# A linear-attention and Fourier-mixing kernel on one core: tiles loaded as 96 and 16 rows, a second copy of half the values, the token fold on VectorE, and a new order of steps

## The chip, the core and the metric

The kernel runs on one core of one Trainium2 chip. Five engines work side by side, each through its own queue in order: TensorE (PE; its weight loads are shown as PEld), VectorE (DVE), ScalarE (ACT), GpSimd (POOL) and SyncE (SP), which here only issues DMAs. They wait for one another by semaphores. The metric is the device time of one execution in microseconds; less is better. Before the change it was 549.24 us, the median of three runs (547.84 to 549.38).

## What is computed

Attention with a decaying state, for 4 batches of 8 heads, 768 tokens and 48 channels:

```python
f = 1.0 / (1.0 + np.exp(-f_logit))
state = np.zeros((B, H, D, D), dtype=np.float32)
for t in range(S):
    state = f[:, :, t, :, None] * state + np.einsum('bhd,bhe->bhde', k[:, :, t], v[:, :, t])
    y[:, :, t] = np.einsum('bhd,bhde->bhe', q[:, :, t], state)
```

The heads' outputs stand beside one another as x (4 x 768 x 384), and the second part is

```python
X = np.fft.fft(np.fft.fft(x, axis=1), axis=2)
u = x + np.real(X)
un = (u - mean(u)) / np.sqrt(var(u) + 1e-06)
return u + np.maximum(un @ w_ch1, 0.0) @ w_ch2
```

with w_ch1 of 384 x 1536 and w_ch2 of 1536 x 384, given as 64-bit floats.

## The kernel before

**Units.** The attention goes by 16 units, each a pair of heads of one batch (unit u is batch u // 4, pair u % 4). A tile of queries, keys or factors has the channels on the partitions and the 768 tokens along the row: one head on rows 0 to 47, the other on rows 64 to 111[...]. Rows 48 to 63 belong to no head; they are filled once (`gap`, L130, and the fills in `start`, L137) so that instructions over all 112 rows read something harmless. The DRAM array holds, for each unit, the two heads' channels one after the other. `load` (L162) brings each tile in as two DMAs of 48 rows. There are four tiles of factors (`g_t`), four of queries (`q_t`) and three of keys (`k_t`), used in turn.

**Steps of a unit** (`attention`, L332, then `outputs`, L511, and `fold`, L613), each ended by a `yield`: (1) exponential and logarithm of the factor on ScalarE; (2) on VectorE a scan over the tokens in six chunks of 128 (L347) and the chunk ends `deep` (L348), of which the sixth column is a copy on GpSimd (L349); (3) three exponentials; (4) queries and keys times decay on VectorE (L359, L361, L362); (5) scores of each chunk's two halves of 64 against themselves, on TensorE (L370); (6) a masked copy (L374); (7) values times these weights, and the far scores, second half of a chunk against the first (L545); (8) the remaining values (L528) and products of keys with values (L565) from keys turned by the word `K` (L507); (9) the scan over chunk states (L573); (10) states into outputs (L582) and five copies; (11) turning back into tokens by channels (L602); (12) and (13) the token fold: sums and differences of token rows that the Fourier part needs.

The far scores of chunks 0 to 2 come out on partitions 0 to 63, those of chunks 3 to 5 on 64 to 127. [...] Before, the halves of chunks 3 to 5 are exchanged for this: in the values by their loads (L169, L171), in the keys by a second multiply that writes in exchanged order (L362).

In `fold` the name `other` (L628) is GpSimd for three units of a batch and VectorE for the fourth; four of the seven operations run on it (L629, L633, L634, L635).

**The Fourier part and the projections.** For each batch b, `F`b steps through the transform (matmuls `z`, L691, and `mix`, L710), `H`b normalizes and turns the rows (L746, L749), and `P`b steps through the two projections: 12 `up` steps (L791) for each pair of row blocks, then the products with w_ch2. For the first pair of batch 0 these are plain (`po`, L800, 8 words); for the other eleven pairs they are seven block products of Strassen's kind (L814). The four combinations of w_ch2's blocks that these need are made once, by the word `W` (`combine`, L317).

**Weights.** The word `r` (or `R`, three at once) issues the load of one block of 64-bit words into one of three `raw` buffers; `C` (`weights`, L286) makes 32-bit floats of it on ScalarE, VectorE (L250, L251) and GpSimd (L252). There are 24 blocks, 12 for each matrix. Later, `V` reads the words of each once more and `c` takes their smallest size. `M` (`judge`, L859) reduces these, and the largest decays, to one flag; at the end every engine loads the flag (L925) and branches (L926): a second, slower way through the whole kernel follows if the numbers demand it, which they don't here.

**What sets the order.** The list `ORDER` is read word by word, and each word issues one step, to all engines that it concerns. An engine's queue thus follows the list. A digit is a unit's next step, `L` with a number and letters a load, `D` eight small matmuls on constant data that only keep TensorE busy, `G` a fill of rows 48 to 63, `I`, `i`, `T`, `S` and `Z` constants and tables.

```python
for word in ORDER.split():
    kind, n = word[0], int("0" + "".join(c for c in word if c.isdigit()))
    if kind.isdigit():
        if n not in units:
            units[n] = attention(n, lambda b=n // HP: x_all(b))
        next(units[n], None)
```

Of the kernel before, what the change touches and what calls it, by code (L numbers as in the profile page):

```python
# [12 lines left out]
C = 128  # L13
# [6 lines left out]
KEEP = 2.0 ** 20  # L20
# [8 lines left out]
    "I D Gq0 D L0f Gk2 D L1f Gk1 D i D 0 Gk0 D D L0v L0q Gq2 D 1 Gq3 0 D 0 Gq1 D L0k 1 D L1q L2f Z D 1 0 "  # L29
    "D 0 2 K0 L1k D 0 0 2 L2q r L2k 1 D 0 0 L3fk 1 2 L1v D 3 0 K1 1 1 L3q 2 L4fk 0 3 1 L2v 2 C 1 4 r r 1 "  # L30
    "K2 2 2 1 0 4 3 C 2 L5fk 3 L3v D D r 5 2 D 3 2 K3 3 1 3 L4qv 5 4 2 L5qv C 3 4 C 4 R 4 3 D T 5 3 5 K4 "
    "2 L6fk C 5 C S 3 2 3 4 K5 r 3 5 4 D C F0 F0 6 F0 4 6 F0 L6qv C 4 6 F0 r 5 4 r H0 H0 L7fk C r 5 H0 6 "
    "7 5 F0 r P0 6 C C 7 L7qv 5 r K6 P0 P0 7 P0 6 C 7 6 C L8fk r r 5 F0 P0 6 r 6 C 8 C P0 L9fk C r P0 7 6 "
    "P0 9 H0 P0 r H0 7 8 7 C r K7 L9qv P0 r 7 9 C 7 9 6 P0 r L8qv 9 P0 C 9 7 9 C K9 C r P0 P0 8 H0 r 8 P0 "
    "r C L10fk 7 9 8 L11qv C L10qv 9 C 9 10 P0 P0 9 H0 P0 P0 5 W P0 6 L11fk P0 P0 P0 8 7 P0 6 P0 P0 P0 4 "
    "10 8 K8 P0 P0 P0 8 11 7 H0 P0 8 P0 P0 P0 P0 10 P0 P0 P0 P0 10 P0 F1 P0 P0 P0 P0 P0 P0 11 11 F1 L12fk "
    "8 10 K10 P0 P0 12 P0 11 10 F1 P0 F1 P0 L12qv L13fk F1 P0 10 11 H1 10 H1 H1 10 F1 P0 12 13 12 P0 P0 "
    "11 P0 P0 P0 P0 P0 P1 F1 8 P1 H1 L13qv K11 10 9 P1 8 P1 12 P1 P1 P1 H1 11 12 11 H1 P1 12 P1 11 9 P1 "
    "13 K12 P1 P1 P1 13 13 P1 10 P1 11 K13 L14fk P1 V L15fk P1 10 11 P1 P1 12 P1 10 13 15 12 H1 P1 P1 P1 "
    "P1 12 P1 12 L14qv H1 P1 11 P1 11 F2 F2 P1 14 14 P1 F2 13 P1 F2 P1 13 F2 P1 13 H2 V P1 P1 P1 15 14 P1 "  # L40
    "P1 P1 P1 P1 P1 c P1 P1 13 P1 14 14 13 K14 P1 V P1 P1 14 P1 F2 P1 14 P1 P1 H2 c P1 c F2 L15qv P1 P1 "
    "P1 P1 P1 P1 15 V P1 H2 V V H2 14 P1 H2 P2 P2 c P2 P2 P2 c P2 15 14 c 12 P2 V V c c P2 P2 P2 14 15 V "
    "V 13 P2 15 V 15 K15 P2 15 H2 P2 P2 P2 V 15 P2 P2 P2 c P2 13 P2 P2 P2 c P2 14 P2 15 H2 14 P2 P2 P2 V "
    "P2 P2 H2 15 P2 P2 P2 P2 P2 P2 P2 P2 14 c V P2 P2 P2 P2 15 12 c P2 c P2 P2 P2 P2 15 P2 V F3 P2 F3 F3 "
    "c P2 V F3 c c P2 F3 P2 P2 F3 P2 F3 P2 H3 P2 P2 P2 P2 P2 H3 P2 H3 H3 H3 P3 P3 P3 P3 P3 P3 P3 P3 P3 P3 "
    "P3 V P3 P3 P3 P3 H3 P3 P3 V P3 P3 c c P3 P3 P3 V V V c P3 P3 P3 P3 P3 P3 P3 P3 c H3 c H3 P3 P3 V P3 "
    "P3 P3 V P3 P3 P3 P3 P3 P3 P3 c c P3 P3 P3 P3 V P3 P3 P3 P3 P3 P3 P3 P3 c P3 P3 P3 P3 P3 P3 M"
# [7 lines left out]
def kernel(  # L55
# [48 lines left out]
    g_t = [fixed([128, S], f"g{i}") for i in range(4)]  # L104
# [25 lines left out]
    def gap(*tiles, value=0.0):  # L130
        for t in tiles:
            nc.vector.memset(t[32:64], value)

    def start():

        for t in g_t:
            nc.gpsimd.memset(t[32:64], 30.0)  # L137
# [24 lines left out]
    def load(u, *names):  # L162
        if u >= B * HP:
            return
        b, hp = divmod(u, HP)
        for name in names:
            if name == "v":
                v_of[u] = p3.tile([128, NCH, 2 * D], F32, tag="v", name=f"v{u}")
                nc.sync.dma_start(out=v_of[u][:, :3], in_=v[b, hp, :, :3])  # L169
                for s in range(2):  # L170
                    nc.sync.dma_start(out=v_of[u][64 * s:64 * s + 64, 3:],  # L171
                                      in_=v[b, hp, 64 - 64 * s:128 - 64 * s, 3:])
                continue
            if name == "V":
                v_of[u] = p3.tile([128, NCH, 2 * D], F32, tag="v", name=f"v{u}")
                nc.sync.dma_start(out=v_of[u], in_=v[b, hp])
                continue
            t, i = {"f": (g_t[u % 4], 2), "k": (k_t[u % 3], 1), "q": (q_t[u % 4], 0)}[name]
            for r in (1, 0):
                nc.sync.dma_start(out=t[ROWS[r]], in_=qkf[b, hp, r, :, i])  # L180
# [117 lines left out]
    def reread():  # L298
        i = len(second)
        t = (k_t[1], g_t[1], k_t[2], g_t[2])[i % 4].bitcast(U32)  # L300
        _, src, cols = blocks_of[i]
        if wide:
            nc.sync.dma_start(out=t, in_=src.bitcast(U32)[:, 2 * cols.start:2 * cols.stop])
        second.append(t.rearrange("p (n w) -> p n w", w=2))
# [27 lines left out]
    def attention(u, x_all):  # L332
# [4 lines left out]
        Q, K, g = q_t[u % 4][:R], k_t[u % 3][:R], g_t[u % 4][:R]  # L337
        AT, AO = at_t[u % 2], ao_t[u % 2]
        at = lambda a, i, c: a.rearrange("p (c t) -> p c t", t=C)[:, c, i]
# [5 lines left out]
        T, ends = deep[:R, u], slice(0, NCH - 1)  # L345
        W = p2.tile([128, S], F32, tag="W", name=f"W{u}")[:R]
        nc.vector.tensor_tensor_scan(W, g, bound[:R], 0.0, ALU.add, ALU.min)  # L347
        nc.vector.tensor_tensor(T[:, ends], at(g, 0, slice(1, NCH)), at(W, C - 1, ends), ALU.add)  # L348
        nc.gpsimd.tensor_copy(T[:, NCH - 1:], W[:, S - 1:S])  # L349
# [4 lines left out]
        te = te_t[u % 2][:R]  # L354
        nc.scalar.activation(te[:, :, ends], T[:, ends].unsqueeze(1).to_broadcast([R, D, NCH - 1]),
# [4 lines left out]
        swap = lambda a: a[:, 3 * C:].rearrange("p (c s t) -> p c s t", c=3, s=2)  # L360
        nc.vector.tensor_tensor(g[:, :3 * C], W[:, :3 * C], K[:, :3 * C], ALU.mult)  # L361
        nc.vector.tensor_tensor(swap(g)[:, :, ::-1], swap(W), swap(K), ALU.mult)  # L362
# [3 lines left out]
        for c in range(NCH):  # L366
            for s in range(2):
                o, k = c * C + 64 * s, c * C + (64 * s if c < 3 else 64 - 64 * s)
                for r in range(2):
                    nc.tensor.matmul(own[64 * s:64 * s + 64, r, c * 64:c * 64 + 64], lhsT=g[ROWS[r], o:o + 64],  # L370
                                     rhs=Q[ROWS[r], k:k + 64], start=True, stop=True)
# [8 lines left out]
    def attention_by_blocks(u, x_all):  # L380
# [5 lines left out]
        Q, K, g = q_t[u % 4][:R], k_t[u % 3][:R], g_t[u % 4][:R]  # L386
# [124 lines left out]
    def outputs(u, x_all, AT, Q, K, te, T=None):  # L511
# [6 lines left out]
        vt = v_of.pop(u)  # L518
        y, vf = y_out, vt.rearrange("p c e -> p (c e)")
# [4 lines left out]
        def values(c, r, rows, t, weights):  # L524
            g, o = into(c, r), c * 2 * D + r * D
# [3 lines left out]
                             lhsT=vf[rows, o:o + (64 if g == 0 else D)], rhs=weights,  # L529
                             start=new, stop=True, skip_group_check=True)  # L530

        def halves(first, second, t, weights):
            for i in range(NCH // 2):
                for p, c in ((first, i), (second, i + 3)):
                    for r in range(2):
                        values(c, r, p, t, weights(p, r, c))

        if te is not None:
            own, far = AT
            halves(hi, lo, hi, lambda p, r, c: own[p, r, c])  # L540
            ps = ps_a.tile([128, 2, 512], F32, tag="sc", name=f"sc{u}_1")
            for i in range(NCH // 2):
                for p, c in ((0, i), (64, i + 3)):
                    for r in range(2):
                        nc.tensor.matmul(ps[p:p + 64, r, i * 64:i * 64 + 64],  # L545
                                         lhsT=K[ROWS[r], c * C + p:c * C + p + 64],
# [9 lines left out]
        else:  # L556
            halves(lo, hi, hi, lambda p, r, c: far[p, r, c % 3])
            halves(lo, hi, lo, lambda p, r, c: own[p, r, c])
# [37 lines left out]
        if te is None:  # L596
            load(u + 4, "q", "V")
# [15 lines left out]
    def fold(u, x):  # L613
# [14 lines left out]
        other = nc.vector if last else nc.gpsimd  # L628
        other.tensor_tensor(f[:, 6:3:-1], x[:, 0:3, ch], x[:, 3:6, ch], ALU.subtract)  # L629
        nc.vector.tensor_tensor(f[:, 1:4], x[:, 0:3, ch], x[:, 3:6, ch], ALU.add)  # L630
        nc.vector.tensor_tensor(f[:, 0:8:7], f[:, 1:7:5], f[:, 2:6:3], ALU.add)
# [386 lines left out]
```

## Time and profile before

| | |
|---|---|
| median of three runs | 549.24 us |
| the profiled execution | 549.43 us |
| its span, first to last instruction | 547.7 us |
| mean granted TensorE clock | 0.969 |
| last TensorE product ends | 537.4 us |

A profile covers one execution. "Busy" is the time in which an engine has an instruction running; the slices give it in tenths for 40 equal parts of the span (13.7 us each). PEclk is the clock that TensorE was granted, as a share of full speed. DMA is the mean busy share of the core's 16 DMA engines. In a row of the timeline stand the start, the duration, the engine, the line of the kernel, the operation, what it writes and reads, how many instructions are merged into the row, and how long the engine had been idle before it and for whom. Two instructions on one engine can overlap a little, so that the distance from start to start can be less than a duration.

DMA bytes and issues of the tiles, from the list of issues: each of `g`, `q` and `k` has 32 DMAs of 144 KB, the values 16 of 144 KB and 32 of 72 KB, the raw weights 24 of 384 KB, with 3.7 to 5.2 us from issue to landing.

### The profile page before, as it was taken

The numbers are of one execution on the slowest core, as the hardware profiler recorded it, in microseconds if no ns is written. First come the engines' busy times: TensorE is split into PE (matmuls) and PEld (weight loads), VectorE is DVE, ScalarE is ACT, GpSimd is POOL, SyncE is SP. The second block draws the span as 40 slices with busy tenths as digits, with TensorE's granted clock in tenths as the row PEclk, the third lists the DMA queues.
The fourth block names the chain that finished last, engine by engine and source line by source line (L and its number), as shares of the span: only waits on it lengthen the run. The fifth ranks groups of instructions, "written<-read, shape, count | busy, mean of one in ns | idle before, by whom it ended". The sixth has DMA issues, their size and how long they took to land.

```text
span 547.7 us, 12758 instructions
## 1 busy us (share of the span) xinstructions
PE 516.5 (94%) x5422; PEld 456.8 (83%) x5422; DVE 292.4 (53%) x534; ACT 200.3 (37%) x529; POOL 99.2 (18%) x149
## 2 busy tenths in 40 slices
PE   6887998999999999999999999999999999999992
PEld 6675777866889899899889899898997888989892
DVE  7859889996754265564354356143264730514141
ACT  6676386873331632443440331413213122030200
POOL 5146634433501000321000000003020000000000
PEclk9888599999999999999999999999999999999997
DMA  7994657776100301213010323202010021120101
GB/s 182 206 240 116 184 137 200 205 216 161 56 4 29 87 4 49 70 42 104 1 30 16 89 87 106 97 1 88 1 57 30 0 82 65 28 89 0 59 0 36
DMA packets 20968, 44.54 MB, mean 81 GB/s; under 512 B 3621, under 2 KB 9318, under 8 KB 20902
## 3 DMA queue, kind: packets, MB, share of 16 engines
q1 hardware_dynamic: 19654, 39.90, 27.2%
q0 software_dynamic: 1104, 3.54, 1.7%
q8 instruction: 44, 0.72, 0.6%
q14 instruction: 22, 0.18, 0.1%
q10 hardware_dynamic: 144, 0.20, 0.1%
HBM read 38.90 MB, written 4.72 MB: 80 GB/s over the span
## 4 chain that ended last, share of the span: by engine, by line
PE 70%; DVE 5%; POOL 1%; DMA 1%; issue 1%; ACT 0%; DVEq 0%; POOLq 0%
PE up L791 29%; PE fx L814 16%; PE fz L814 12%; PE z L691 3%; PE mix L710 2%; PE y L528 2%; PE pt L749 1%; PE y L582 1%; DMA raw<-in_w_ch_dram 1%; PE yt L602 1%; PE po L800 1%; PE ds L565 1%; PE sc L370 1%; PE st L507 1%; DVE w L251 1%
## 5 line engine op out<-in xcount | busy, mean ns | idle before, releaser
L791 PE MATMUL up<-unT,w 128*128 128x256 f32 x864 | 195.6, 381 | 1.4 <-DVE x L769 1.1
L791 PEld LDWEIGHTS up<-unT,w 128*128 128x128 f32 x864 | 161.4, 190 | 23.0 <-PE up L791 1.1
L793 ACT ACTIVATE h<-up 128x256 f32<-128x256 f32 x144 | 54.9, 383 | 177.1 <-PE up L791 162.4
L658 POOL DMA_INDIRECT out_dram<-x,place x16 | 16.6, 1038 | 219.7 <-DVE x L844 166.3
L821 DVE TENSOR_TENSOR s<-h,h 128x768 f32<-128x768 f32 x11 | 10.5, 955 | 67.6 <-ACT h L793 67.6
L814 PE MATMUL fx<-block,h 128*128 128x192 f32 x264 | 46.5, 326 | 0.0
L814 PE MATMUL fx<-w,h 128*128 128x192 f32 x264 | 44.9, 326 | 0.0
L814 PEld LDWEIGHTS fx<-w,h 128*128 128x128 f32 x264 | 43.3, 190 | 0.3
L814 PEld LDWEIGHTS fx<-block,h 128*128 128x128 f32 x264 | 43.5, 190 | 0.0
L252 POOL TENSOR_TENSOR w<-w,raw 128x384 uint32<-128x384 uint32 x24 | 28.4, 1183 | 36.3 <-ACT raw L248 16.9
L347 DVE TENSOR_TENSOR_SCAN W<-g,bound 112x768 f32<-112x768 f32 x16 | 28.0, 1753 | 12.9 <-ACT g L341 12.4
L374 DVE COPY_PREDICATED at<-causal,sc 128x768 f32<-128x768 uint32 x16 | 16.6, 1040 | 18.8 <-PE sc L370 18.6
L814 PE MATMUL fz<-block,h 128*128 128x192 f32 x132 | 23.3, 327 | 0.1
L814 PE MATMUL fz<-w,s 128*128 128x192 f32 x132 | 23.3, 327 | 0.0
L814 PE MATMUL fz<-w,h 128*128 128x192 f32 x132 | 23.3, 327 | 0.0
L750 ACT COPY unT<-pt 128x384 f32<-128x384 f32 x24 | 11.5, 483 | 30.3 <-PE pt L749 30.3
L528 PE MATMUL y<-at,v 64*48 64x64 f32 (+1 forms) x768 | 19.6, 235 | 2.5 <-DVE at L374 1.5
L359 DVE TENSOR_TENSOR q<-q,g 112x768 f32<-112x768 f32 x16 | 16.9, 1054 | 9.5 <-ACT g L352 9.5
L814 PEld LDWEIGHTS fz<-block,h 128*128 128x128 f32 x132 | 21.7, 190 | 0.3 <-PE fx L814 0.3
L349 POOL COPY deep<-W 112x1 f32<-112x1 f32 x16 | 5.5, 344 | 89.7 <-DVE W L347 89.7
L814 PEld LDWEIGHTS fz<-w,h 128*128 128x128 f32 x132 | 21.7, 190 | 0.0
L814 PEld LDWEIGHTS fz<-w,s 128*128 128x128 f32 x132 | 21.7, 190 | 0.0
(152 smaller groups left out, 785.7 us busy)
## 6 DMA issues: line engine op xcount, KB each, us to landing
raw<-in_w_ch_dram SPq DMA_DIRECT2D x24, 384.0 KB, 4.5
g<-in_qkf_dram SPq DMA_DIRECT2D x32, 144.0 KB, 4.0
q<-in_qkf_dram SPq DMA_DIRECT2D x32, 144.0 KB, 5.2
k<-in_qkf_dram SPq DMA_DIRECT2D x32, 144.0 KB, 4.8
k<-in_w_ch_dram SPq DMA_DIRECT2D x12, 384.0 KB, 4.1
g<-in_w_ch_dram SPq DMA_DIRECT2D x12, 384.0 KB, 3.4
v<-in_v_dram SPq DMA_DIRECT2D x16, 144.0 KB, 3.7
v<-in_v_dram SPq DMA_DIRECT2D x32, 72.0 KB, 3.9
```

What stands on the lines that cost most here:

```text
L252: nc.gpsimd.tensor_tensor(bits, bits, lo, ALU.add)
L347: nc.vector.tensor_tensor_scan(W, g, bound[:R], 0.0, ALU.add, ALU.min)
L359: nc.vector.tensor_tensor(Q, Q, g, ALU.mult)
L374: nc.vector.copy_predicated(AT, causal[:, :64].bitcast(U32).unsqueeze(1).unsqueeze(1).to_broadcast([128, 2, NCH, 64]), own[:, :, :NCH * 64 ...
L528: nc.tensor.matmul(y[FILL[g], c // 3, c % 3 * C + t.start:c % 3 * C + t.stop], lhsT=vf[rows, o:o + (64 if g == 0 else D)], rhs=weights, st ...
L658: nc.gpsimd.indirect_dma_start(out=out.rearrange("b s d -> (b s) d"), out_offset=bass.IndirectOffsetOnAxis(ap=place[:, b, i:i + 1], axis=0 ...
L691: nc.tensor.matmul(z[:, cols], lhsT=src[:, j, lo:hi], rhs=tab[:, t, T % 2, cols], start=(i == 0), stop=(i == len(parts) - 1), skip_group_c ...
L710: nc.tensor.matmul(mix[:, o], lhsT=zz[:rows_of[T], T, PLACES[c]], rhs=cd[:rows_of[T], T, :NQ - odd], start=(i == 0), stop=(i == 1))
L750: nc.scalar.copy(turned[j][:, :, t], pt[:, :DM].rearrange("p (k t) -> p k t", k=3))
L791: nc.tensor.matmul(pp[:, :256], lhsT=w1[:, kt, m * 128:(m + 1) * 128], rhs=unT[:, kt], start=(kt == 0), stop=(kt == 2))
L793: nc.scalar.activation(hs[-1][:, m % H].rearrange("p t n -> p (t n)"), pp[:, :256], AF.Relu)
L814: nc.tensor.matmul(out, lhsT=h[:, m], rhs=blocks[i][:, m], start=(start and m == 0), stop=(m == H - 1), skip_group_check=True)
```

## The change

- Each tile of queries, keys and factors is loaded as one DMA of 96 rows (both heads, without a gap, on rows 0 to 95) and one of 16 rows: the second head's first 16 channels once more, on rows 96 to 111. The second head is then read on rows 64 to 111, with its channels in another order, the same in queries, keys and factors. The fills of the gap and the word `G` are gone.
- The factor tiles get one more column, a zero, so that VectorE makes all six columns of `deep` in one instruction.
- Values are loaded whole, and rows 0 to 63 of chunks 3 to 5 a second time to partitions 64 to 127 of a tile `vx` (three buffers). The exchanged order is gone, and one multiply over 768 tokens stands for two of 384.
- All seven operations of the token fold run on VectorE for every unit.
- `ORDER` is another list. It has the same words but for the seven `G`.

```diff
-    g_t = [fixed([128, S], f"g{i}") for i in range(4)]
+    g_t = [fixed([128, S + 1], f"g{i}") for i in range(4)]
...
-            nc.gpsimd.memset(t[32:64], 30.0)
+            nc.gpsimd.memset(t[:, S:], 0.0)
...
-                v_of[u] = p3.tile([128, NCH, 2 * D], F32, tag="v", name=f"v{u}")
-                nc.sync.dma_start(out=v_of[u][:, :3], in_=v[b, hp, :, :3])
-                for s in range(2):
-                    nc.sync.dma_start(out=v_of[u][64 * s:64 * s + 64, 3:],
-                                      in_=v[b, hp, 64 - 64 * s:128 - 64 * s, 3:])
-                continue
...
+                v_of[u] = (p3.tile([128, NCH, 2 * D], F32, tag="v", name=f"v{u}"),
+                           pr.tile([128, NCH // 2, 2 * D], F32, tag="vx", name=f"vx{u}"))
+                nc.sync.dma_start(out=v_of[u][0], in_=v[b, hp])
+                nc.sync.dma_start(out=v_of[u][1][64:], in_=v[b, hp, :64, 3:])
...
-            for r in (1, 0):
-                nc.sync.dma_start(out=t[ROWS[r]], in_=qkf[b, hp, r, :, i])
+            rows = qkf.rearrange("b h r d i s -> (b h r d) i s")
+            first = 2 * D * u
+            nc.sync.dma_start(out=t[:2 * D, :S], in_=rows[first:first + 2 * D, i])
+            nc.sync.dma_start(out=t[2 * D:R, :S], in_=rows[first + D:first + 64, i])
...
-        nc.vector.tensor_tensor(T[:, ends], at(g, 0, slice(1, NCH)), at(W, C - 1, ends), ALU.add)
-        nc.gpsimd.tensor_copy(T[:, NCH - 1:], W[:, S - 1:S])
+        nc.vector.tensor_tensor(T, g_t[u % 4][:R, C::C], W[:, C - 1::C], ALU.add)
...
-        swap = lambda a: a[:, 3 * C:].rearrange("p (c s t) -> p c s t", c=3, s=2)
-        nc.vector.tensor_tensor(g[:, :3 * C], W[:, :3 * C], K[:, :3 * C], ALU.mult)
-        nc.vector.tensor_tensor(swap(g)[:, :, ::-1], swap(W), swap(K), ALU.mult)
+        nc.vector.tensor_tensor(g, W, K, ALU.mult)
...
-                                         lhsT=K[ROWS[r], c * C + p:c * C + p + 64],
+                                         lhsT=K[ROWS[r], c * C:c * C + 64],
...
-            halves(lo, hi, hi, lambda p, r, c: far[p, r, c % 3])
-            halves(lo, hi, lo, lambda p, r, c: own[p, r, c])
+            for i in range(NCH // 2):
+                for p, c in ((lo, i), (hi, i + 3)):
+                    for r in range(2):
+                        values(c, r, p, hi, far[p, r, i], moved=c >= 3)
+            diagonal(lo, hi)
...
-        other = nc.vector if last else nc.gpsimd
-        other.tensor_tensor(f[:, 6:3:-1], x[:, 0:3, ch], x[:, 3:6, ch], ALU.subtract)
...
+        tt = nc.vector.tensor_tensor
+        tt(f[:, 6:3:-1], x[:, 0:3, ch], x[:, 3:6, ch], ALU.subtract)
```

`diagonal` is `halves` for the scores of a half against itself; `moved` makes `values` take the second copy.

The list up to the middle of batch 0's projections, before:

```
I D Gq0 D L0f Gk2 D L1f Gk1 D i D 0 Gk0 D D L0v L0q Gq2 D 1 Gq3 0 D 0 Gq1 D L0k 1 D L1q L2f Z D 1 0
D 0 2 K0 L1k D 0 0 2 L2q r L2k 1 D 0 0 L3fk 1 2 L1v D 3 0 K1 1 1 L3q 2 L4fk 0 3 1 L2v 2 C 1 4 r r 1
K2 2 2 1 0 4 3 C 2 L5fk 3 L3v D D r 5 2 D 3 2 K3 3 1 3 L4qv 5 4 2 L5qv C 3 4 C 4 R 4 3 D T 5 3 5 K4
2 L6fk C 5 C S 3 2 3 4 K5 r 3 5 4 D C F0 F0 6 F0 4 6 F0 L6qv C 4 6 F0 r 5 4 r H0 H0 L7fk C r 5 H0 6
7 5 F0 r P0 6 C C 7 L7qv 5 r K6 P0 P0 7 P0 6 C 7 6 C L8fk r r 5 F0 P0 6 r 6 C 8 C P0 L9fk C r P0 7 6
P0 9 H0 P0 r H0 7 8 7 C r K7 L9qv P0 r 7 9 C 7 9 6 P0 r L8qv 9 P0 C 9 7 9 C K9 C r P0 P0 8 H0 r 8 P0
r C L10fk 7 9 8 L11qv C L10qv 9 C 9 10 P0 P0 9 H0 P0 P0 5 W P0 6 L11fk P0 P0 P0 8 7 P0 6 P0 P0 P0 4
...
```

and after:

```
L0f Z L1f I 0 D D L0q D 0 i D 1 1 D 0 L2f L0k 0 D D D r L0v D D C L1q D 2 D L2k 0 D L1k D 1 0 2 1 r
0 L2q K0 C L3fk 0 D 0 1 2 D 1 2 3 0 3 2 2 L4fk L1v 4 K1 r 1 4 C 1 1 L3q 3 0 1 L2v K2 3 r 2 L3v 1 0 3
C 2 L5fk 3 D 5 D D 2 4 L4qv 2 R K3 2 3 1 D 3 4 2 3 4 3 2 5 L5qv 4 3 L7fk T 5 4 3 S K4 7 D 3 L6fk C r
4 4 C F0 r F0 F0 5 F0 C 4 F0 K5 5 H0 5 H0 C r 4 5 H0 L7qv C r C r r F0 L6qv 6 F0 5 C P0 6 C P0 P0 P0
5 r 6 P0 P0 5 6 C 6 K6 r C P0 r H0 C 6 r P0 P0 P0 7 r C P0 6 r H0 C r P0 6 C 7 H0 r P0 C r 7 6 C r C
P0 7 6 7 K7 r P0 L9fk L8qv C L9qv 7 C 6 L8fk C 7 5 P0 9 4 5 9 P0 P0 7 8 P0 P0 9 P0 P0 8 8 L10fk P0 9
7 9 L10qv K9 H0 P0 P0 8 P0 9 P0 P0 P0 9 8 9 H0 9 L11fk P0 W P0 9 K8 8 10 P0 11 10 P0 11 8 7 P0 8 6
...
```

The old list ends in `P3 P3 P3 M`; the new one in `c M` and thirteen more `P3`.

## The prediction

> **What bounds the kernel now.** I read the page's busy shares and slices first, then busy time by stage, then the timeline at the stage borders, then the last ten microseconds.
>
> ```profile
> span 547.7 us, 12758 instructions
> ...
> PE 516.5 (94%) x5422; PEld 456.8 (83%) x5422; DVE 292.4 (53%) x534; ACT 200.3 (37%) x529; POOL 99.2 (18%) x149
> ...
> PE   6887998999999999999999999999999999999992
> ...
> DVE  7859889996754265564354356143264730514141
> ...
> PEclk9888599999999999999999999999999999999997
> DMA  7994657776100301213010323202010021120101
> ```
>
> TensorE (PE) is full from slice 9 on; before that VectorE (DVE) shows 8 and 9, the DMA 9, and the granted clock dips to 5.
>
> ```profile
> core 0: us, PE busy (x) PEld busy (x) DVE busy (x) ACT busy (x) POOL busy (x), PEclk, DMA share, GB/s
> 0.00:118.00 118.00, 100.29 (x1922) 83.32 (x1923) 101.33 (x164) 79.64 (x191) 53.42 (x88) 0.88 0.75 186
> 118.00:154.00 36.00, 34.97 (x420) 26.20 (x419) 28.23 (x47) 14.27 (x34) 14.02 (x18) 1.00 0.43 116
> 154.00:537.00 383.00, 380.57 (x3080) 347.17 (x3078) 161.05 (x315) 106.39 (x306) 31.74 (x44) 1.00 0.15 47
> 537.00:548.00 11.00, 0.70 (x4) 0.11 (x3) 1.77 (x9) 0.00 (x0) 0.00 (x0) 0.68 0.13 45
> ...
> 40.00:52.00 12.00, 8.62 (x262) 7.20 (x259) 10.51 (x16) 8.52 (x19) 7.74 (x10) 0.89 0.42 104
> 52.00:67.00 15.00, 13.95 (x214) 11.25 (x215) 13.30 (x27) 5.62 (x14) 9.49 (x15) 0.52 0.62 186
> 67.00:84.00 17.00, 15.63 (x270) 12.68 (x269) 15.14 (x31) 12.90 (x42) 6.63 (x10) 1.00 0.62 157
> ```
>
> From 118 to 537 us TensorE idles 3.5 us of 419, so the end can move only by what is lost before 118 us, or by the tail after 537. From 40 to 84 us VectorE is busy 38.95 of 44 us: it sets the pace there.
>
> To see what is lost I gave every step of the list a price, start to start, from the timeline at full clock. TensorE: own scores 0.93 us, first values and far scores 0.84, second values and state products 1.65, state into outputs 0.83, turning back 0.72, keys turned 0.63, `D` 0.6, `z` or `mix` 1.31, one tile turned 0.49, an `up` step 1.30, a `po` or Strassen product 1.95. VectorE: scan and ends 1.87, multiplies 2.0, masked copy 0.97, state scan 0.7, a weight block 0.87, combine 5.5. All TensorE steps come to 505.4 us; the last product ends at 537.4, so 32.0 us are lost. Where, by three marks:
>
> ```profile
> 40.50 0.95 PE L370 MATMUL sc<-q,g 48*64 48x64 f32 x48
> ...
> 80.65 1.46 PE L791 MATMUL up<-unT,w 128*128 128x256 f32 x6
> ...
> 130.59 5.97 PE L800 MATMUL po<-w,h 128*128 128x384 f32 x18
> ```
>
> Own scores of unit 3 start at 40.5 us with 26.6 us of steps listed before them, the first `up` at 80.65 with 53.9, the last `po` ends at 136.5 with 106.5. Lost: 13.9, 26.75 and 30.0 us. VectorE's sums before the first two are 29.6 and 65.2.
>
> The tail:
>
> ```profile
> 537.36 0.56 DVE L848 TENSOR_TENSOR x<-fx,x 128x384 f32<-128x384 f32 x1 [1.59 <-PE fx L814]
> ...
> 539.60 0.14 DVE L873 TENSOR_SCALAR flag<-most 1x1 int32<-1x1 f32 x1
> ...
> L925 PEldq TENSOR_LOAD <-flag x1: 493/493/493, 539.8 to 539.8; - x1
> ...
> L926 PEldq COMPARE_BRANCH  x1: 3442/3442/3442, 540.4 to 540.4; - x1
> ```
>
> All five engines load the flag at 539.8, the moment it is written; TensorE's branch then takes 3.44 us, and the span ends 3.8 us after it.
>
> [...] 12.6 to 29.5 us, mostly 48-row loads, moved 214 GB/s at a share of 1.04; 98 to 105 us, mostly 128-row weights, 245 at 0.88. [...] Here a 0.36 us L631 took 1.38 at 142.15 us beside a GpSimd L635. [...] The clock of 0.52 from 52 to 67 us agrees with a half clock[...].
>
> **The change part by part.**
>
> *Tail.* The check `M` stands 13 `P3` words earlier, so its VectorE chain (537.8 to 539.74) and its matmul fall beside the last products; its wait stands in TensorE's queue behind an `up`, when VectorE has nothing else listed. The flag is old when the engines come to load it. TensorE can load it at 537.3 in place of 539.8: -2.5; its branch still ends at about 541.2. ScalarE, whose last store is issued until 539.05, is there by 539.6. I take -2.6. Floor of the gain 1.8 (only VectorE's chain goes), ceiling 4 (TensorE's sequencer branches under the last matmuls).
>
> *Fills.* Seven `G` fills (0.70 us each, VectorE) and four GpSimd fills go. Six of the seven stood beside the wait for the first load and its exponentials (the scan starts at 6.20, `ln` ends at 6.11), so they give nothing; the seventh delayed the second scan: -0.6. If that cover were gone they would be worth 3.7.
>
> *Loads.* Each query, key and factor tile moves 336 KB for 288, in two issues as before; values 369 KB for 295 in two issues for three. No row shows a 96-row load. Two 48-row loads take 288/214 = 1.35 us of the queue. [...] Upper: 96 rows as two loads and the 16 rows as dear as a third, 2.02. I take 1.35, no difference.
>
> *Token fold.* Twelve units lose L629, L633, L634, L635 on GpSimd (842, 940, 297, 781 ns) and get them on VectorE, as every fourth unit has them now (447, 260, 200 and 347 ns): a fold is 2.33 us of VectorE for 1.14, so 1.19 more, and no wait for GpSimd. Behind it wait the next scan and weight block, in order. Before the first `up` three folds (units 0, 1, 2) become dearer: +3.6. [...] Later folds stand beside a full TensorE.
>
> *Multiplies.* L361 and L362 (604 + 658 ns) become one of 112x768; L359 of that shape takes 1054: -0.15 to -0.2 each, six before the first `up`: about -1. *Sixth deep column:* one GpSimd copy (344 ns) off, no VectorE instruction added: 0. The far scores keep their 24 matmuls.
>
> *The list.* TensorE's total is unchanged. Sums before the marks, with these prices: own scores of unit 3: TensorE 23.2 (26.6 before), VectorE 26.2 (29.6). First `up`: TensorE 55.3 (53.9), VectorE 62.7 (65.2). Last `po`: 98.6 (106.5). VectorE's work between the first two is 36.5 us (35.6), which took 40.15.
>
> Now the times. First mark: taking off six hidden fills and adding nothing, VectorE is level (26.2 against 25.9), so 40.8. But before, VectorE idled 3.46 us at 29.9 for the state products of unit 1, whose TensorE chain ran at clock 0.57; the new list puts two scans and a masked copy ahead of that wait and unit 2's own scores ahead of unit 1's outputs. I take half: 39.1. Then 36.5 of work plus the 4.5 that 35.6 cost beyond itself[...]: 78.5 us at the first `up`. Lost there: 78.5 - 55.3 = 23.2 against 26.75, so -3.5.
>
> From the first to the last `po` TensorE lost 3.3 us; the new list has less else to do there (43.3 us of TensorE for 52.6). Eleven weight blocks go through the three `raw` buffers in it, ten of them in 23.4 us of TensorE work. Before, ten took 27.9 (97.67 to 125.53 on GpSimd), four in a row 9.33. So 0 to 4.5 us may be lost; I take 3.3 again, and the same 2.0 to the end.
>
> **Sum.** The profiled execution took 549.43 us (span 547.7 and 1.7 around it). -3.5 - 2.6 gives 543.3. It lay 0.19 above the median of the three runs; against that, 543.2.
>
> **The rivals.**
>
> *A, the sum above:* 543.2, own range 539 to 547. Chance 0.43.
>
> *B, only the tail:* the first 80 us are round trips between engines, and a better list moves the same waits elsewhere. For it: VectorE is 11 us behind its own sum already at 40 us. Against: 40 to 84 us is 88% VectorE. 549.2 - 2.6 = 546.6, 545 to 548.5. Chance 0.18.
>
> *C, the cold spell goes too:* between 49 and 70 us the clock was about 0.55[...]. Without it, some 7 us more (21 us at 0.57 mean is 9 of lost clock, part of it under VectorE): 536, 533 to 539. Against: the new list has its `D` fillers at much the same distances. Chance 0.14.
>
> *D, slower: the loads.* From 7 to 42 us the DMA share is 0.97 to 1.06, so any byte added is time. The new list also draws two weight blocks (393 KB each) forward, and puts their VectorE steps ahead of the masked copy of unit 0 and the state scan of unit 0; VectorE, in order, waits there for them. If a load costs the upper 2.02 us, the 14 tiles listed up to unit 3's scores land 14 x 0.67 = 9.4 us later and the front gains nothing: 549.2 - 2.6 + 6.5 (about 3 us are slack) = 553. It decides once a 96 + 16 load costs over 1.75 us, where 5.6 - 3 eats the tail's gain. Chance 0.25.
>
> That the kernel doesn't do what it says has little room: its instructions stand in the code as described.
>
> **How the numbers follow.** About 0.3%, 1.65 us, is what a measurement of this kernel tells from no change. Faster: 0.41 of A, 0.10 of B, C: 0.65. Same: 0.02 of A, 0.08 of B, 0.02 of D: 0.12. Slower: 0.23. The range leaves out most of D above 552 and little of C below 534: 534 to 552.
>
> **What would show it.** Right: the flag loads at 537 to 538 us on TensorE; first `up` near 78.5 and own scores of unit 3 near 39; VectorE up by some 11 us and GpSimd down by 35 in busy time. Wrong: TensorE idle before 118 us not under 17 us; SP or VectorE waiting on `g`, `k`, `q` or `raw` loads for several us before 42; a cold spell longer than 21 us.

## The result, and the profile after

The changed kernel takes 544.26 us in the median of seven runs (542.17 to 545.93); the kernel before, beside it, 549.24 (547.38 to 552.11). The ratio is 0.990, 95% interval 0.9865 to 0.9935: 5 us less. The profiled execution took 542.37 us, near the low end of its runs, so a mark in its trace can stand some 2 us earlier than in a usual run. A line number is that of the kernel spoken of; in the changed one most lines stand some 8 earlier than before.

First the page of the changed kernel (called "after" from here on): the shares of busy time, then the slices (13.5 us each).

```profile
span 540.6 us, 12660 instructions
...
PE 513.1 (95%) x5422; PEld 454.4 (84%) x5422; DVE 291.9 (54%) x559; ACT 201.1 (37%) x529; POOL 56.3 (10%) x85
...
PE   6787989989999999999999999999999999999995
...
DVE  4878889958397344378442554255473142513231
...
PEclk9879889999999999999999999999999999999999
DMA  8997275588220320101201302204101007200001
```

GpSimd lost 43 us of work, VectorE gained none (291.9 for 292.4), and the dip of the clock to 5 around 55 us is gone. By stage (columns as before):

```profile
0.00:118.00 118.00, 99.83 (x1867) 82.60 (x1868) 91.96 (x158) 76.78 (x181) 39.22 (x69) 0.93 0.72 200
118.00:154.00 36.00, 36.00 (x441) 29.25 (x440) 25.78 (x38) 18.78 (x45) 2.24 (x1) 1.00 0.52 143
154.00:534.00 380.00, 377.30 (x3117) 342.60 (x3115) 173.65 (x364) 105.50 (x303) 14.87 (x15) 1.00 0.16 50
```

TensorE's idle time before 118 us is about what it was (18.2 us for 17.7), but it has more of its list done by then. From the timeline, the three marks of the prediction: own scores of unit 3, first `up`, last run of `po`.

```profile
37.32 0.93 PE L359 MATMUL sc<-q,g 48*64 48x64 f32 x48
...
79.36 1.53 PE L783 MATMUL up<-unT,w 128*128 128x256 f32 x6
...
117.02 8.65 PE L792 MATMUL po<-w,h 128*128 128x384 f32 x26 [1.43 <-POOL w L244]
```

With the prediction's prices, 14.1, 24.1 and 27.1 us are lost at these marks, for 13.9, 26.75 and 30.0 before. The last product ends at 534.0 us, for 537.4. And the tail, from the instructions on the line of the flag's load (L914) and on the line of the branch (L915). In these rows a "q" behind the engine's name stands for its sequencer; the three durations are in ns, then come the first and the last start in us:

```profile
L914 PEldq TENSOR_LOAD <-flag x1: 488/488/488, 530.9 to 530.9; - x1
...
L914 DVEq TENSOR_LOAD <-flag x1: 792/792/792, 534.0 to 534.0; - x1
L914 ACTq TENSOR_LOAD <-flag x1: 478/478/478, 536.1 to 536.1; - x1
...
L915 PEldq COMPARE_BRANCH  x1: 3998/3998/3998, 531.5 to 531.5; - x1
...
L915 ACTq EVENT_SEMAPHORE  x1: 17/17/17, 539.4 to 539.4; - x1
```

TensorE's sequencer begins its branch (4.0 us) while TensorE still works on the last products, and is through at 535.5, 1.5 us behind the last of them. ScalarE, which issues the last store, is now the last to come. From the last product to the end of the span there are 6.6 us, before 10.3.

### The profile page after: what moved, and what is told of

It reads as the page before. It is cut to its first block, busy times and chain, and to the rows that moved or that the text cites. A ratio compares the mean times of both kernels' runs of the same rounds, so it can differ in the third digit from the quotient of the medians.

```text
span 540.6 us, 12660 instructions
## 1 busy us (share of the span) xinstructions
PE 513.1 (95%) x5422; PEld 454.4 (84%) x5422; DVE 291.9 (54%) x559; ACT 201.1 (37%) x529; POOL 56.3 (10%) x85
## 4 chain that ended last, share of the span: by engine, by line
PE 82%; DVE 7%; DMA 5%; POOL 2%; issue 2%; ACT 1%; SPq 0%; DVEq 0%; POOLq 0%
PE up L783 32%; PE fx L806 16%; PE fz L806 12%; DMA raw<-in_w_ch_dram 3%; PE y L517 3%; PE z L683 3%; PE mix L702 2%; PE ds L557 2%; PE sc L359 2%; PE y L574 2%; PE y L151 2%; DMA wave<-in_dim_tab_dram 2%; PE po L792 2%; PE yt L594 1%; PE pt L741 1%
## 5 line engine op out<-in xcount | busy, mean ns | idle before, releaser
L650 POOL DMA_INDIRECT out_dram<-x,place x16 | 17.1, 1070 | 399.6 <-DVE x L836 298.1
L565 DVE TENSOR_TENSOR_SCAN stt<-ds,te 112x288 f32<-112x288 f32 x16 | 12.0, 751 | 38.7 <-PE ds L557 38.7
L244 POOL TENSOR_TENSOR w<-w,raw 128x384 uint32<-128x384 uint32 x24 | 26.2, 1094 | 57.2 <-DVE w L243 32.0
L517 PEld LDWEIGHTS y<-at,v 64*48 64x48 f32 (+1 forms) x768 | 15.5, 136 | 6.1 <-issue 2.7
```

Of the source, the lines that this page charges most:

```text
L244: nc.gpsimd.tensor_tensor(bits, bits, lo, ALU.add)
L517: nc.tensor.matmul(y[FILL[g], c // 3, c % 3 * C + t.start:c % 3 * C + t.stop], lhsT=vals[rows, o:o + (64 if g == 0 else D)], rhs=weights, ...
L565: nc.vector.tensor_tensor_scan(flat(st[:R]), ps[:R, 0, :NCH * D], flat(te), 0.0, ALU.add, ALU.mult)
L650: nc.gpsimd.indirect_dma_start(out=out.rearrange("b s d -> (b s) d"), out_offset=bass.IndirectOffsetOnAxis(ap=place[:, b, i:i + 1], axis=0 ...
```

## The experiments

All ratios are to the kernel before, measured on the same chip in the same session, with 95% intervals; its median was 547.3 to 548.6 us there, so 0.001 is 0.55 us.

**The tail alone, and the rest alone.** In the kernel before, only `M` moves (and what it needs ahead of it); in the changed kernel, only `M` goes back.

```diff
-... V c c P3 P3 P3 P3 V P3 P3 P3 P3 P3 P3 P3 P3 c P3 P3 P3 P3 P3 P3 M      (before)
+... V c c P3 P3 P3 P3 P3 c M P3 P3 P3 P3 P3 P3 P3 P3 P3 P3 P3 P3 P3       (b_M_early)
...
-P3 P3 P3 P3 c P3 P3 P3 c M P3 P3 P3 P3 P3 P3 P3 P3 P3 P3 P3 P3 P3         (after)
+P3 P3 P3 P3 c P3 P3 P3 c P3 P3 P3 P3 P3 P3 P3 P3 P3 P3 P3 P3 P3 M         (a_M_end)
```

> The kernel before with one word of its list moved: the check M stands thirteen P3 earlier (with the last V and c ahead of it), as in the new list; nothing else changes. Theory 1 (the tail is its own share, the front another): the stretch from the last product to the end falls from 10.3 us to the 6.6 of the changed kernel, so -3.7 us, 545.5 us beside 549.2, ratio 0.993. Rival (all of the gain is the tail): the whole -5.0, 544.3 us, ratio 0.991. Rival (the tail is worth what the forecast took): -2.6, 546.6, ratio 0.995.

> The changed kernel with M put back to the end of its list. Theory 1: +3.7 us, 548.0 us, ratio 0.998 to the kernel before, which leaves -1.3 for everything but the tail. Rival (all of it is the tail): 549.2, ratio 1.000. Rival (the front is worth the 3.4 us that the profiles show, and the tail less): 546.5, ratio 0.995.

Measured: `b_M_early` 0.9948 (0.9921 to 0.9975), -2.85 us; `a_M_end` 0.9959 (0.9938 to 0.9979), -2.25 us. Their product, 0.9907, agrees with the ratio of the whole change (0.990), so within the intervals the two shares add up. That all of the gain is the tail is refuted by `a_M_end`, whose interval ends below 1. The tail's value lies between 1.4 and 4.3 us; the interval excludes neither the 2.6 of the forecast nor the 3.7 of the traces. The trace of `b_M_early` shows the same picture as after:

```profile
L925 PEldq TENSOR_LOAD <-flag x1: 488/488/488, 536.7 to 536.7; - x1
...
L926 PEldq COMPARE_BRANCH  x1: 3822/3822/3822, 537.3 to 537.3; - x1
```

Its last product ends at 539.7 us; the branch is through at 541.1. In the traces of all kernels with `M` last, 9.6 to 10.4 us follow the last product, in all with `M` early 6.3 to 7.0.

The two traces also tell how far a mark of one profile can be trusted: `b_M_early` is the kernel before up to the last pair, yet its first `up` starts at 83.1 us, not 80.65; `a_M_end` has it at 81.5, not 79.4.

**The instructions alone, the list alone.** `ops_only` is the changed kernel under the list of before without the seven `G`; `list_only` is the kernel before under the new list, with `I` and the seven fills ahead of it.

```diff
 # ops_only: the changed kernel with
-ORDER = (the new list)
+ORDER = (the list of before, without G)
 # list_only: the kernel before with
-ORDER = (the list of before)
+ORDER = (I Gq0 Gk0 Gk1 Gk2 Gq1 Gq2 Gq3, then the new list without I)
```

> The changed kernel's instructions (96 and 16 rows, second copy of values, fold and sixth column on VectorE, one multiply) under the list of before without its seven G words, M at the end. Theory 1 (the operations are about neutral): 548 to 550 us, ratio 0.998 to 1.002; loads faster, fold dearer by 1.2 us for each unit but fewer waits for GpSimd. Rival (the faster loads bring the front's gain): 546 to 547.5, ratio 0.995 to 0.997. Rival (the fold on VectorE costs the front its time and the new list pays it back): 551 to 553, ratio 1.004 to 1.007.

> The instructions of before under the new list; the constants I and the seven fills G stand ahead of the first load, since a load must follow the fill. Theory 1 (tail and order of steps carry the gain): 544 to 545.5 us, ratio 0.990 to 0.993. Rival (the new list needs the new instructions: GpSimd's fold or the 48-row loads hold it up): 547 to 550, ratio 0.996 to 1.002. Rival (only the tail): 545.5, with the first up step no earlier than 80 us.

Measured: `ops_only` 1.0051 (1.0032 to 1.0071), 2.8 us slower; `list_only` 0.9955 (0.9931 to 0.9978). Neither came as Theory 1 had it; `list_only` fits its last rival, the tail only (545.4 us, and its trace has the first `up` at 82.0). `list_only` includes the early `M`; divided by `b_M_early`, its front is 1.0007, with some 0.0036 either way: no gain that can be told. (The fills and constants ahead of its list are in that; what they cost is measured below, under the changed instructions.) But under the changed instructions the same list is worth much: `a_M_end` to `ops_only`, both with `M` last, is 0.9908, with some 0.003 either way, so 5 us. So the front's gain is neither the list's alone nor the instructions' alone; it needs both.

The trace of `list_only` shows one place where they meet. This is TensorE's longest wait before 160 us, but for the one at the very start (total, times, longest), and then GpSimd's timeline:

```profile
PE z L691 <- POOL tab L208: 3.8, 1, 3.8
```

```profile
50.58 0.19 POOL L349 COPY deep<-W 112x1 f32<-112x1 f32 x1 [2.69 <-DVE W L347]
...
51.55 1.85 POOL L193 DMA_INDIRECT tab<-in_seq_tab_dram,back  x1 [0.30 <-DMA tab<-in_seq_tab_dram]
59.45 0.27 POOL L207 COPY pair<-tab 128x8 f32<-128x8 f32 x1 [6.05 <-DMA tab<-in_seq_tab_dram,back]
```

The word `T` puts a table's load into GpSimd's queue. With the folds in that queue (the last ends at 47.9 us), and behind them the copy of the sixth column, for which GpSimd waited 2.7 us on VectorE, it was issued at 51.55 us, and the first transform step waited 3.8 us for the table. In the changed kernel GpSimd was free of both:

```profile
40.58 1.15 POOL L185 DMA_INDIRECT tab<-in_seq_tab_dram,back  x1 [0.30 <-POOL back L184]
```

That is 11 us earlier, and no transform step `z` waited for the table. Whether this one place is the whole of it, the next two runs were to tell.

**The fold alone, under both lists.** L621, L625, L626 and L627 go back to GpSimd in three units of four.

```diff
-        tt(f[:, 6:3:-1], x[:, 0:3, ch], x[:, 3:6, ch], ALU.subtract)
+        other = nc.vector if last else nc.gpsimd
+        other.tensor_tensor(f[:, 6:3:-1], x[:, 0:3, ch], x[:, 3:6, ch], ALU.subtract)
...
-        nc.vector.tensor_copy(f[:, 1:7:5], f[:, 0:8:7])
+        other.tensor_copy(f[:, 1:7:5], f[:, 0:8:7])
...
```

> The changed kernel with the token fold as before: four of its seven operations on GpSimd in three units of four. Under the old list the changed kernel's instructions cost 2.8 us, under the new one they gain some 3, so something in them needs the new list. Theory 1 (it is the fold: the new list leaves VectorE room for it): 547 us, near the 0.9955 that the new list gives with the old instructions. Rival (the fold is neutral, the loads matter): 544, ratio 0.990, as the changed kernel. Rival (the fold on VectorE costs its 1.2 us for each of the three early units also here): 541 to 542, ratio 0.985.

> The changed kernel's instructions but for the fold (GpSimd has its four operations again, in three units of four), under the list of before, M at the end. All of the changed instructions there took 2.8 us more than before. Theory 1 (the fold's extra work on VectorE, 3.6 us before the first up step, is that loss): 547 us, ratio 0.998 to 1.000. Rival (loads, values and the merged multiply are the loss): 550, ratio 1.004 to 1.006. Rival (the loads gain and the fold alone loses more): 545, ratio 0.994 to 0.997.

Measured: 0.9937 (0.991 to 0.9964) under the new list, 1.0046 (1.0014 to 1.0078) under the old. The second is level with `ops_only` (1.0051), so the fold isn't the loss there. The first lies between the two values that were set against each other, and its interval reaches 0.9955 and the changed kernel's 0.990: undecided between the first two theories. The third is outside it: the fold on VectorE doesn't cost the new list time. VectorE had 281.6 us of work with the fold on GpSimd for 291.9, and in its trace the first `up` came no earlier (80.5 us). The table's load was issued there at 52.3 us, as late as in `list_only`, but TensorE reached the transform only at 60.5 us and waited 0.8 us. So the late table is a cost in one trace, and not shown to be the whole.

**The loads alone.** `a_96_fills` is the changed kernel with the old fills and `I` ahead of the list, as in `list_only`; `a_48_rows` differs from it in the loads alone.

```diff
-            nc.sync.dma_start(out=t[:2 * D, :S], in_=rows[first:first + 2 * D, i])
-            nc.sync.dma_start(out=t[2 * D:R, :S], in_=rows[first + D:first + 64, i])
+            nc.sync.dma_start(out=t[ROWS[1], :S], in_=rows[first + D:first + 2 * D, i])
+            nc.sync.dma_start(out=t[ROWS[0], :S], in_=rows[first:first + D, i])
```

> The changed kernel with the fills of rows 32 to 63 that the old loads needed and the constants put ahead of the first load; the loads stay 96 and 16 rows. It is the control of a_48_rows, and tells the cost of the fills: Theory 1 (hidden but for the one that held the second scan, 0.6 us): 544 to 545 us, ratio 0.990 to 0.992. Rival (the fills and constants hold the first loads up): 546 to 548, ratio 0.994 to 0.998.

> The changed kernel with each tile of queries, keys and factors loaded as two DMAs of 48 rows and the gap filled, constants and fills ahead of the first load. Beside a_96_fills, which has the same fills, it tells the loads alone. Theory 1 (forecast: the two kinds of load are level): equal to a_96_fills within 0.7 us. Rival (96 and 16 rows are faster[...]): 2 to 3 us more than a_96_fills, ratio 0.995 to 0.998.

Measured: 0.9928 (0.9902 to 0.9953) and 0.9933 (0.991 to 0.9955). The loads are level (0.3 us apart, with some 1.9 either way). What the fills cost here can't be told from nothing: beside 0.990, `a_96_fills` is 1.5 us slower, with some 2.4 either way. Two views bear on why faster transfers brought nothing; after stands in them for `a_96_fills`, whose profile caught its longest execution (548.66 us). From 7 to 42 us, in `a_48_rows` and then after (the last numbers are the clock, the DMA share and GB/s):

```profile
7.00:42.00 35.00, 30.85 (x718) 26.91 (x715) 27.37 (x39) 24.86 (x51) 8.13 (x19) 0.80 0.96 235
```

```profile
7.00:42.00 35.00, 28.73 (x715) 25.25 (x712) 27.41 (x39) 26.52 (x53) 5.58 (x8) 0.85 0.97 260
```

At the same share of busy engines the 96-row loads move 11% more bytes, but a tile has 17% more (336 KB for 288). And TensorE's waits for which no releaser is found ("issue"), again `a_48_rows` and then after:

```profile
PE y L579 <- issue: 1.9, 1, 1.9
...
PE ds L562 <- issue: 1.4, 1, 1.4
...
PE y L522 <- issue: 0.5, 2, 0.3
```

```profile
PE ds L557 <- issue: 2.1, 1, 2.1
...
PE y L574 <- issue: 1.7, 1, 1.7
...
PE y L517 <- issue: 1.1, 1, 1.1
```

Summed up to 160 us they are 2.7 to 3.8 us in the six traces with 48-row loads, 4.6 to 7.3 in the eight with 96-row loads. What TensorE waits for in most of them is, by what follows, its own instructions. The page of this kernel has 44 packets and 0.72 MB on a queue of the kind "instruction", 16.4 KB each.

Most of these waits stand at fixed counts of instructions, and end soon after such a packet. TensorE's recorded instructions (matmuls, weight loads and those of its sequencer) were counted up to each of the 49 such waits of 0.25 us or more that the fourteen traces have before 160 us. In 41 of them the count is 193 or a multiple of 256 more, and each of these 41 waits ends 1.2 to 1.7 us after one of the 16-KB packets has ended. In the trace of after, for one, TensorE stands from 39.5 to 41.7 us at count 1473, which is 193 and five times 256, and the packet runs from 39.0 to 40.15. The other eight waits are at other counts, and their cause stays open. That the 96-row loads make the stalls longer is so in these traces; what the stalls cost in the time was not measured apart.

**The clock.** Before, TensorE idled 2.06 us at 46.5 us, and a clock of 0.5 followed from 50 to 66 us. `b_warm` fills that window with four more `D`; `a_warm` fills three later windows of the changed kernel with five.

```diff
-L5qv C 3 4 C 4 R 4 3 D T
+L5qv C 3 4 C D D D D 4 R 4 3 D T          (b_warm)
...
-L5qv 4 3 L7fk T 5 4 3 S ... K5 5 H0
+L5qv 4 D D 3 L7fk T 5 D 4 3 S ... K5 5 D D H0   (a_warm)
```

> The kernel before with four more words D (thirty-two small matmuls on constant data, about 2.4 us at full clock) ahead of unit 4's own scores, where TensorE idled 2.06 us at 46.5 us for the multiplies; a clock of about 0.5 from 50 to 66 us followed. Nothing else changes, M stays last. Theory 2 (that cold spell is a cause of the time before 80 us: TensorE's work there at half clock holds the front up, and the new list is faster since its idle windows there are shorter): the spell goes, and 2 to 4 us with it, 543.7 to 545.7 us beside 547.7, ratio 0.993 to 0.996. Rival (VectorE sets the pace there, and TensorE's clock is hidden under it): the spell goes and the time stays, ratio 0.999 to 1.001. Rival (the fillers only push the own scores back): slower by 0.5 to 1, ratio 1.001 to 1.002.

> The changed kernel with five more words D where TensorE still idled between 50 and 72 us: two ahead of the turning back at 52.5 us (idle 1.15), one ahead of the values at 54.0 (0.75), two ahead of the first turned tile at 71.1 (1.57). Theory 2 (cold clock costs time): the short spells at 54 to 58 and 72 to 75 us go, and 1 to 2 us with them: 542.5 us beside 547.7, ratio 0.988 to 0.990. Rival (hidden under VectorE, or the spells come from instruction fetches earlier, which no filler helps): as the changed kernel, 0.990 to 0.992. Rival (the fillers stand in the way): 0.993 to 0.995.

Measured: `b_warm` 1.0094 (1.0064 to 1.0125), 5 us slower, which no theory had; `a_warm` 0.9903 (0.9866 to 0.994), as the changed kernel. The fillers did not take the cold spell away (the clock of `b_warm` was 0.5 from 50 to 62 us), so this run doesn't tell what the spell costs. In `a_warm` one of the two short spells went and one stayed (70.0 to 73.4 us), and its interval covers more than one of its theories. The 5 us of `b_warm` have a cause that can be seen. Its first `up` came early, at 78.1 us, but from there to the last product it took 4.2 us more than the kernel before (460.9 for 456.7). At 121.5:

```profile
121.08 0.43 PE L566 MATMUL ds<-v,kT 128*64 128x48 f32 x7
124.11 1.01 PE L566 MATMUL ds<-v,kT 128*48 128x48 f32 x13 [2.60 <-issue]
```

In the middle of one step TensorE stood 2.6 us without instructions, and its clock fell to a half for 3.4 us after that: 0.88 and 0.90 as the means of these two stretches, where the kernel before has 1.00.

```profile
118.00:126.00 8.00, 5.40 (x173) 4.46 (x172) 3.79 (x7) 4.09 (x8) 4.04 (x4) 0.88 0.95 217
126.00:134.00 8.00, 8.00 (x43) 4.77 (x42) 3.59 (x7) 1.42 (x6) 2.18 (x3) 0.90 0.40 112
```

The test of it: the same four fillers in the same place, but taken from elsewhere, so that the count of instructions is the old one from 64 us on.

```diff
-L5fk 3 L3v D D r 5 2 D 3 2 ... C 3 4 C 4 R 4 3 D T ... 4 D C F0
+L5fk 3 L3v D r 5 2 3 2 ... C 3 4 C D D D D 4 R 4 3 T ... 4 C F0
```

> The kernel before with four of its own words D moved and none added: two from 39 to 40 us, one from 50.6 and one from 64.2 us to just ahead of unit 4's own scores (46.5 us). From 64 us on TensorE has issued as many instructions as in the kernel before. With four words added instead, the first up step came 2.6 us earlier and yet the time was 5 us longer: TensorE stood 2.6 us without instructions at 121.5 us, and its clock fell after it. Theory 3 (a stall for instructions falls at fixed counts of instructions, and is long where the DMA queues are loaded; added words shift it): no such stall from 110 to 140 us, as in the kernel before, and the time is level or better, 544 to 548 us beside 547.3, ratio 0.994 to 1.001. Rival (the fillers themselves, or an earlier first up step that meets the weight loads, cost the time): 551 to 552.5, ratio 1.006 to 1.010.

Measured: 0.9995 (0.997 to 1.002). The stall is gone and the clock stays at 1.00:

```profile
118.00:126.00 8.00, 7.96 (x183) 5.67 (x182) 6.07 (x10) 4.69 (x10) 3.80 (x4) 1.00 1.00 224
126.00:134.00 8.00, 8.00 (x46) 4.79 (x45) 5.91 (x9) 1.42 (x6) 2.18 (x3) 1.00 0.52 150
```

So 64 more instructions (32 matmuls and their weight loads) cost far more than their own 2.4 us (four `D` at the 0.6 of the prediction), by where in the list the later counts then fall. The count says the same: the stall of `b_warm` stands at count 4289, which is 193 and sixteen times 256. In the kernel before and in `b_warm_moved` this count is reached 64 instructions later in the list, behind a dozen products with w_ch2 of 0.49 us each; the packet had ended 2.2 and 1.5 us earlier, and TensorE didn't stand. That such stalls are long where the DMA queues are loaded fits two traces, before and then after, and was not tested apart: up to 160 us, at a DMA share of 0.65 and 0.66, the waits without a releaser come to 2.7 and 4.9 us; from there to the end of the products, at 0.15 and 0.16, to 0.2 and 1.3. That the filler's place costs the time is refuted. That an early first `up` costs it is not tested apart: in `b_warm_moved` it came at 79.4 us, not 78.1.

The record says something more on what a cold spell is worth. TensorE up to the end of its last product, before and then after:

```profile
0.00:537.40 537.40, 516.14 (x5420) 456.70 (x5420) 290.67 (x526) 200.29 (x529) 99.19 (x149) 0.97 0.30 82
```

```profile
0.00:534.00 534.00, 513.13 (x5422) 454.44 (x5422) 291.39 (x558) 201.06 (x529) 56.33 (x85) 0.98 0.31 89
```

The idle time is all but the same (21.3 and 20.9 us); 3.0 of the 3.4 us by which the last product ends earlier are busy time. It is the same work, with 27.3 us of it at half clock before and 17.1 after. And of the 174 executions of the kernel before that stand beside the experiments, each with its mean clock on record, those with more time at half clock took longer, by 0.31 us for each us (0.27 to 0.35, within a session). That is a connection and not a cause shown: what holds TensorE up can also lower its clock (it fell after steps with 0.8 to 2.3 us of work in 3.41, as the last section has it), and no run changed the clock alone. Against it stands `list_only`: 19.6 us at half clock in its median execution for 27.8 in `b_M_early` (worked out from the mean clocks), and the time is level.

**The fills under the old list.**

```diff
 # ops_keep_fills: the changed kernel with the fills of before (GpSimd's four in start, gap and G) and
-ORDER = (the new list)
+ORDER = (the list of before, whole)
```

> The changed kernel's instructions under the whole list of before, its seven G words and the four GpSimd fills kept, so that they start as before did: the matmuls D, which need no fill, no longer begin early. Without the fills this list took 2.8 us more than before, with the fold on GpSimd 2.5 more. Theory 1 (the loss is the start: the fills gone, the D words run out sooner and TensorE idles and cools at 7 to 21 us instead of later): back to 547 to 548.5, ratio 0.999 to 1.001. Rival (the loss is in the merged multiply, the values' loads or the 96-row loads under the old list): 549.5 to 551, ratio 1.003 to 1.006.

Measured: 1.0107 (1.007 to 1.0144), neither theory: worse than without the fills (1.0051), so under the old list, with the changed instructions, the fills cost some 3 us (0.8 to 5.4) where the forecast had 0.6. Its trace has the longest "issue" stalls of all, 7.3 us, and its first transform step at 69.7 us for 65.0 before. Why the changed instructions lose under the old list is thus not settled; longer stalls beside the 96-row loads are in its traces (4.7 us in `ops_only` for 2.7), but the new list bears the same stalls (4.9 us after) without a loss.

## Why the prediction was right, point by point

- *The time* (543.2 us) came out at 544.26, within the own range of case A, 539 to 547. The two shares were mis-sized in opposite directions, if the middles of the intervals are taken: the front -2.25 (1.15 to 3.4) for a forecast -3.5, the tail -2.85 (1.4 to 4.3) for -2.6. Within the front, in the traces, the own scores of unit 3 came 1.8 us earlier than forecast (37.3 for 39.1), and the stretch from there to the first `up` took 42.0 us for 39.4. That the sum came so near is in part luck: its parts hold less well.
- *The signs.* Of those that were to show the prediction right, the first `up` (79.4 us for 78.5) and GpSimd's fall (43 us for 35) came, the flag's load and VectorE's busy time did not. And one of those that were to show it wrong came: TensorE's idle time before 118 us is 18.2 us, not under 17. (SyncE's waits on `raw` loads before 42 us, which were another, are 4.1 us, but were 3.9 before; a cold spell of over 21 us did not come.) The front's gain isn't in the idle time in these traces, but in the busy time.
- *Tail.* The flag's load was forecast at 537.3 us, with the branch behind the last product. It came at 530.9, 3 us ahead of that product's end, and most of the branch ran under the products: what the prediction gave as its ceiling. What comes last now is ScalarE, behind its store.
- *Fills:* -0.6 forecast; under the new list `a_96_fills` can't be told from none, under the old one they are worth some 3 us, near the 3.7 that the prediction gave them if nothing covered them. *Sixth column* (0 forecast) was not measured apart. *`raw` buffers:* from the first `up` to the last `po` TensorE lost 3.0 us more (27.1 less 24.1), forecast 3.3; 1.9 us of waits for converted weight blocks are in it, the longest 1.43.
- *Loads:* level, as taken; rival D (slower, 553) falls with it. At the rates from 7 to 42 us a tile takes about the same (1.3 us each way, an estimate from 344,000 bytes at 260 GB/s and 295,000 at 235). The longer stalls for instructions beside the 96-row loads are a term that the prediction didn't have; what they cost is not shown. (The prediction mixes KB of 1000 and of 1024 bytes; its 1.35 us would be 1.38.)
- *Token fold:* +3.6 less 1.6 forecast on the way to the first `up`; the 78.5 us there have both in them. The 1.6 was the author's estimate from before: L359 at 46.39 us took 1.34 us for a median of 0.95, and L631 and L644 waited 0.68 and 0.48 for GpSimd. No such cost was found under either list. With the fold on GpSimd VectorE had 56.6 us of work in the first 80 for 61.4, and the first `up` came no earlier: in these two traces VectorE's sum doesn't set the pace there.
- *VectorE up by 11 us of busy time* was wrong: it fell by 0.5. The sum left out what goes in the same rows. The fold brings 14.3 (12 times 1.19), but the seven fills take 4.9, sixteen merged multiplies (998 ns for 604 and 658) 4.2, and L350, L626 and L636 are 4.8 shorter in all: before, single rows of theirs were long (three of L359 with 1.34 to 1.77 us for a median of 0.95, one of L644 with 2.21 for 0.46, one of L634 with 1.53 for 0.20), each while GpSimd worked on the fold or on a weight block (L252). The prediction had counted the fills as gone, but not in this sum.
- *Multiplies:* -0.26 us each for -0.15 to -0.2.
- *The list* carried the front by itself in the prediction. Alone it brings none of it, and the instructions alone cost 2.8 us; together they gain. The step that failed is to price the list with VectorE's sums and the instructions with theirs, and to add. One term that this leaves out is visible: the folds and the sixth column stood ahead of the tables in GpSimd's queue. What else the list and the instructions need each other for stays open.
- *Rival B* (only the tail, 546.6) is refuted by `a_M_end`. *Rival C* (the cold spell between 49 and 70 us goes): most of it did (3.4 us at half clock there for 17.1), and the 7 us that it was to bring did not come (the view of that stretch before has a mean clock of 0.59, not 0.57). At half clock, in the trace of before, the own scores of a unit took 1.56 us (at 55.04) for 0.95 at full clock (at 40.50), and the turning back 1.38 (at 56.53) for 0.79 (at 44.12). What such a spell costs is open; the figures above allow some 0.3 us for each us.

## What to carry to other kernels

A new order and new instructions are tuned to each other: measure both alone before giving either the credit. Put the last decision that all engines wait for ahead of the last long work, not behind it, even if every engine is idle at the end: the sequencer's own branch then runs under that work. And when a small edit early in a long kernel moves the time by far more than its own length, look for waits without a releaser later on, count the engine's instructions up to them, and test with an edit that keeps that number.

## What the runs showed of the hardware

- TensorE's branch takes 3.3 to 4.2 us in the fourteen traces, the other engines' 50 to 72 ns, at a time when the DMA queues are nearly idle (a share of 0.07 from 540 to 544 us before). In each of the fourteen a 16-KB packet of the instruction queue runs within it, and the branch ends 1.3 to 1.5 us after that packet; by this, what the branch waits for is a block of instructions.
- TensorE stalls for instructions at fixed counts, every 256 of its instructions, 0.3 to 3.3 us each where it stalls at all. The same place (`ds` near 42 us) took 1.4, 2.0, 2.1, 2.6 and 3.3 us in five traces of the new list; 2.1 and 3.3 are after and `a_M_end`, the same program up to there. So this alone can make executions of one kernel differ by a microsecond.
- Such a stall can lower the clock afterwards (a half for 3.4 us after 2.6 us in `b_warm`), so that it costs more than it lasts. Not each does: none followed the stall of 2.1 us in the trace of after.
- TensorE's clock changes in steps of 3.41 us: in the trace of before its stretches at one clock, from 22 to 66.4 us, last 6.83, 6.83, 3.41, 10.24 and 17.07 us. Up to 170 us the fourteen traces have 43 falls to a half; in the step ahead of each TensorE was busy for 0.8 to 2.3 us. The 523 steps at full clock that no fall follows have 1.84 us or more. So TensorE needn't be idle through a whole step for its clock to fall: here it always fell with less than 1.8 us of work in a step, and never with more than 2.3. In `b_warm` the step ahead of the long spell still had only 1.8, in spite of the fillers.
